# Sliding-window attention plus MLP on one core: attention in 64-key blocks on partition halves, 448 contracted as seven 64-row halves, a fixed queue order

## The chip, the cores and the metric

The kernel runs on one core of one Trainium2 chip. The metric is the device time of one execution in microseconds (us), lower is better. Each kernel was executed several times; "span" is the time from the first to the last instruction of the profiled execution, which lies 1.7 to 1.9 us under that execution's time where the record gives both. A run is called slow when it lies more than 1.5% above the fastest run of the same kernel; on one core nothing else tells such a run apart.

## The reference, cut to what matters

There are 2048 tokens of width 448 in bf16 and 16 heads of 28. Each query attends to eight keys: its own position and those 2, 4, ..., 14 behind it. So even and odd tokens never meet in attention. An MLP with token shifts of 1 and 2 follows, then a second MLP of width 1792.

```python
def _A_ref(x, wqkv, wo):                 # called with layernorm(x); H = 16, Dh = 28
    W, dil = 8, 2
    q, k, v = ...                        # x @ wqkv, split by heads
    idx = pos[:, None] - off[None, :]    # off = 0, 2, ..., 14
    logits = einsum("bhsd,bhswd->bhsw", q, kg) * Dh ** -0.5     # kg, vg gathered by idx
    attn = softmax(where(mask, logits, -1e9))
    return einsum("bhsw,bhswd->bhsd", attn, vg) @ wo

def _B_ref(x, w1, w2, w3, w4):           # called with layernorm(h)
    h = gelu(layernorm(x) @ w1)
    hs = concat(shift(h, quarters, by +1, -1, +2, -2)) @ w2
    x1 = x + hs
    return x1 + gelu(layernorm(x1) @ w3) @ w4      # w3: 448 x 1792, w4: 1792 x 448

h = x + _A_ref(layernorm(x), wqkv, wo)
out = h + _B_ref(layernorm(h), w1, w2, w3, w4)
```

## The kernel before

Tokens are cut into four tiles of 512 tokens of one parity. The contraction of 448 is four chunks of 112 rows, so each 512-column product is four matmuls that use 112 of the 128 rows. Attention works in blocks of 110 keys and 103 queries: five blocks per tile and head. The program first makes a graph of operations; a greedy list scheduler then decides, when the program is built, which operation each engine queue takes next.

```python
    def phase_QK(t):                     # phase_V is alike, 110 tokens a block
        for c in range(4):
            T = tile(2)
            for which in range(2):
                for kc in range(4):      # 4 x 112 rows
                    j0 = 16 * which + 4 * c
                    mm(T(...), wqk_p[:, kc, j0:j0 + 4, :]..., hT[0:KC, par, kc, :], kc == 0, kc == 3, 512)
            copy(qk[:, par, c, :, 8:520], T(...), 1024)

    def phase_att(t):
        for c in range(4):
            for jp in range(2):
                T = tile(2)
                for q0, nq, k0 in BLK:                        # five blocks of 103 queries, 110 keys
                    for j in (2 * jp, 2 * jp + 1):
                        mm(T(...), qk[32 * j:32 * j + 28, par, c, 1, k0:k0 + KB],
                           qk[32 * j:32 * j + 28, par, c, 0, 8 + q0:8 + q0 + nq], True, True, nq, "rows")
                pj = pt[0:KB, sl, 2 * jp:2 * jp + 2, :]
                act(pj, T(...), ACT.Exp, 1024, scale=SCALE)
                dve("tensor_tensor", 1024, 2.0, out=pj, in0=pj, in1=m_, op=ALU.mult)     # mask
            ...                                                # attention times V, 20 matmuls; evacuation
        # softmax denominators: gathered, inverted, stored, broadcast by DMA
        dma("zg%d" % par, zp[:, par, :], zrows, 32768)
        dve("reciprocal", 400, out=rzp[:, par, :], in_=zp[:, par, :])
        ...
        dma("zs%d" % par, zd..., rzp[:, par, :], 32768)
        for j in range(4):
            dma("zb%d" % j, rzb[32 * j:32 * j + 32, :, :]..., bass.AP(rz_d, ...), 32 * 8192)
        for c in range(4):
            dve("tensor_tensor", 512, out=oT[:, par, c, :], in0=osb[:, par, c, :], in1=rzb[:, c, :], op=ALU.mult)

    def schedule(self, dma_bw=180.0, slack=100.0):
        ...
        while done < n:                  # of all ready operations take the one that can start first
            for e in engs:
                for op in ready[e]:
                    st = max(avail(op, e), fr)
                    ...
                    if cand is None or st < cand[0] - slack or (st < cand[0] + slack and op.prio < cand[1].prio):
                        cand = (st, op)
```

## Time and profile before

| | before |
|---|---|
| median of 3 runs (lowest, highest) | 247.87 us (245.72, 248.72) |
| span of the profiled execution | 245.1 us |
| TensorE, VectorE, ScalarE busy | 205.1, 119.4, 122.3 us |
| matmuls | 1505 |
| bytes moved by DMA | 19.82 MB |

The page's first lines give busy time per engine. The rows of tenths cut the span into 40 slices of 6.1 us: 9 is 90% busy or more. PEclk is the clock granted to TensorE, in tenths. The trace's first clock record lies at 19.3 us here, and the page counts the time before it as full clock; the 9s at the head of this row are therefore no measurement. The q8 line is a queue whose packets the page calls instruction, 14 of them here.

```profile
PE 205.1 (84%) x1505; PEld 104.5 (43%) x1505; DVE 119.4 (49%) x237; ACT 122.3 (50%) x138; POOL 61.7 (25%) x123
PE   0389787899799759659782999999999999999990
PEclk9999979999999967959997699999999999999999
DMA  6910598950700774447044400046000401001110
...
q8 instruction: 14, 0.23, 0.4%
```

The groups of instructions, by form. After the count stand the total busy time in us, the mean of one in ns, then the engine's idle time just ahead and what ended it.

```profile
L1181 PE MATMUL ps<-hT,arena 112*128 112x512 bf16 x128 | 30.5, 395 | 1.0 <-ACT pt L1181 0.9
L1181 ACT ACTIVATE pt<-ps 110x1024 bf16<-110x1024 f32 x32 | 30.3, 1037 | 0.3 <-PE ps L1181 0.3
L1181 DVE TENSOR_TENSOR pt<-pt,msk 110x1024 bf16<-110x1024 bf16 x32 | 21.8, 697 | 12.0 <-ACT pt L1181 11.8
L1181 PE MATMUL ps<-qk 28*110 28x103 bf16 (+1 forms) x320 | 11.5, 227 | 6.4 <-ACT pt L1181 2.5
```

Matmuls overlap: one of the first line takes 395 ns on average, yet 25 of them from 48.91 us on start 216 ns apart and take 5.57 us in all. So a matmul's mean is not its pace: pace is the distance between starts. What TensorE waited for, by who released it, in us in total, times, longest:

```profile
PE ps L1181 <- ACT lntm L1181: 8.7, 3, 6.8
PE ps L1181 <- DVE oT L1181: 6.0, 5, 3.9
PE ps L1181 <- ACT pt L1181: 5.6, 10, 1.4
PE ps L1181 <- DMA actT<-lntm: 2.9, 2, 2.5
```

The timeline of TensorE at the two ends of what matters here (start in us, length in us, what, count, idle before it):

```profile
13.76 5.96 PE L1181 MATMUL ps<-arena,hT 112*110 112x448 bf16 x16 [1.11 <-ACT hT L1181]
...
135.27 17.44 PE L1181 MATMUL ps<-actT,w_s 112*128 112x512 bf16 x72 [2.52 <-DMA actT<-lntm]
```

"issue" is the page's word for a wait that nothing in the profile explains. TensorE's first large product (V of the first tile) starts at 13.76 us and runs at 5.96/16 = 372 ns a matmul, where the same form later takes 202 ns (3.23 us for 16 at 41.97 us). And between there and 135 us TensorE stands idle again and again for other engines, while from 135.27 us on it is nearly gapless.

### The profile page before, as it was taken

The numbers are of one execution on the slowest core, as the hardware profiler recorded it, in microseconds if no ns is written. First come the engines' busy times: TensorE is split into PE (matmuls) and PEld (weight loads), VectorE is DVE, ScalarE is ACT, GpSimd is POOL, SyncE is SP. The second block draws the span as 40 slices with busy tenths as digits, with TensorE's granted clock in tenths as the row PEclk, the third lists the DMA queues.
The fourth block names the chain that finished last, engine by engine and source line by source line (L and its number), as shares of the span: only waits on it lengthen the run. The fifth ranks groups of instructions, "written<-read, shape, count | busy, mean of one in ns | idle before, by whom it ended". The sixth has DMA issues, their size and how long they took to land.

```text
span 245.1 us, 3658 instructions
## 1 busy us (share of the span) xinstructions
PE 205.1 (84%) x1505; PEld 104.5 (43%) x1505; DVE 119.4 (49%) x237; ACT 122.3 (50%) x138; POOL 61.7 (25%) x123
## 2 busy tenths in 40 slices
PE   0389787899799759659782999999999999999990
PEld 0245333545445544415341354544454454445550
DVE  6456872165677797778799100773036122002221
ACT  2635865677955795861836565154615600650000
POOL 8830835010000500320539100286003600000000
PEclk9999979999999967959997699999999999999999
DMA  6910598950700774447044400046000401001110
GB/s 165 282 49 19 111 221 249 299 86 8 175 5 11 174 84 88 100 91 177 17 73 86 86 0 0 3 92 136 0 19 3 86 19 56 3 1 39 37 61 26
DMA packets 31671, 19.82 MB, mean 81 GB/s; under 512 B 24800, under 2 KB 30256, under 8 KB 31136
## 3 DMA queue, kind: packets, MB, share of 16 engines
q1 hardware_dynamic: 30608, 15.10, 29.0%
q0 software_dynamic: 1040, 4.42, 6.6%
q8 instruction: 14, 0.23, 0.4%
q14 instruction: 9, 0.07, 0.1%
HBM read 11.65 MB, written 1.97 MB: 56 GB/s over the span
## 4 chain that ended last, share of the span: by engine, by line
PE 61%; ACT 12%; DVE 10%; POOL 6%; DMA 6%; issue 2%; DVEq 0%
PE ps L1181 61%; ACT pt L1181 5%; DMA actT<-lntm 3%; DVE st L1181 3%; POOL rstd L1181 3%; DMA hT<-lntm 3%; ACT lntm L1181 3%; DVE oT L1181 2%; ACT arena L1181 2%; DVE xb L1181 2%; POOL nmr L1181 1%; ACT qk L1181 1%; ACT vt L1181 1%; DVE mv L1181 1%; DVE pt L1181 1%
## 5 line engine op out<-in xcount | busy, mean ns | idle before, releaser
L1181 PE MATMUL ps<-actT,w_s 112*128 112x512 bf16 (+1 forms) x288 | 65.5, 387 | 2.9 <-DMA actT<-lntm 2.9
L1181 ACT ACTIVATE arena<-ps 128x1024 bf16<-128x1024 f32 (+1 forms) x35 | 35.9, 1025 | 42.7 <-PE ps L1181 42.6
L1181 DVE TENSOR_TENSOR xb<-ps,xb 128x448 bf16<-128x448 f32 (+1 forms) x24 | 18.5, 771 | 75.0 <-PE ps L1181 75.0
L1181 PEld LDWEIGHTS ps<-actT,w_s 112*128 112x128 bf16 (+1 forms) x288 | 30.3, 107 | 35.8 <-DMA actT<-lntm 3.4
L1181 PE MATMUL ps<-w_s,arena 128*128 128x448 bf16 x224 | 43.0, 352 | 0.0
L1181 PE MATMUL ps<-hT,arena 112*128 112x512 bf16 x128 | 30.5, 395 | 1.0 <-ACT pt L1181 0.9
L1181 PEld LDWEIGHTS ps<-w_s,arena 128*128 128x128 bf16 x224 | 21.9, 98 | 20.6
L1181 ACT ACTIVATE pt<-ps 110x1024 bf16<-110x1024 f32 x32 | 30.3, 1037 | 0.3 <-PE ps L1181 0.3
L1181 POOL TENSOR_SCALAR vtmp<-mv 128x4 f32<-128x4 f32 (+1 forms) x19 | 3.8, 198 | 94.9 <-DVE mv L1181 93.9
L1181 DVE TENSOR_TENSOR pt<-pt,msk 110x1024 bf16<-110x1024 bf16 x32 | 21.8, 697 | 12.0 <-ACT pt L1181 11.8
L1181 PE MATMUL ps<-wo_s,oT 128*128 128x448 bf16 x64 | 17.2, 415 | 6.5 <-DVE oT L1181 6.0
L1181 PEld LDWEIGHTS ps<-hT,arena 112*128 112x128 bf16 x128 | 12.6, 101 | 16.5 <-issue 2.0
L1181 DVE BATCH_NORM_STATS2 st<-xin 128x6 f32<-128x448 bf16 x32 | 19.2, 599 | 0.5 <-issue 0.5
L1181 POOL TENSOR_TENSOR rstd<-vtmp,mhalf 128x4 f32<-128x4 f32 (+1 forms) x19 | 18.3, 962 | 1.6
L1181 PE MATMUL ps<-arena,hT 112*110 112x448 bf16 x64 | 15.6, 407 | 2.5 <-ACT qk L1181 1.4
L1181 PE MATMUL ps<-qk 28*110 28x103 bf16 (+1 forms) x320 | 11.5, 227 | 6.4 <-ACT pt L1181 2.5
L1181 POOL TENSOR_TENSOR xb<-xb,xin 128x448 bf16<-128x448 bf16 x16 | 16.2, 1040 | 2.3 <-ACT lntm L1181 1.7
L1181 ACT ACTIVATE lntm<-xin,nmr,rstd 128x448 bf16<-128x448 bf16 x16 | 11.3, 752 | 10.5 <-POOL nmr L1181 10.5
L1181 ACT ACTIVATE qk<-ps 128x1024 bf16<-128x1024 f32 x10 | 10.1, 1021 | 10.7 <-PE ps L1181 10.7
L1181 PEld LDWEIGHTS ps<-wo_s,oT 128*128 128x128 bf16 x64 | 6.7, 110 | 16.4 <-DVE oT L1181 8.8
L1181 ACT ACTIVATE lntm<-xb,nmr,rstd 128x448 bf16<-128x448 bf16 x11 | 7.7, 751 | 12.0 <-POOL nmr L1181 12.0
L1181 PEld LDWEIGHTS ps<-qk 28*110 28x110 bf16 x320 | 8.9, 134 | 10.7 <-ACT pt L1181 3.8
(58 smaller groups left out, 172.2 us busy)
## 6 DMA issues: line engine op xcount, KB each, us to landing
rzb<-rz_scratch SPq DMA_DIRECT2D x16, 256.0 KB, 4.6
w_s<-in_B_w_dram POOLq DMA_DIRECT2D x2, 1568.0 KB, 11.2
out_dram<-xb SPq DMA_DIRECT2D x16, 112.0 KB, 1.7
xin<-in_A_x_dram SPq DMA_DIRECT2D x3, 448.0 KB, 8.0
arena<-in_A_wqkv_dram SPq DMA_DIRECT2D x3, 392.0 KB, 5.5
w_s<-in_B_w_dram POOLq DMA_DIRECT2D x2, 392.0 KB, 7.5
xin<-in_A_x_dram SPq DMA_DIRECT2D x4, 112.0 KB, 2.2
wo_s<-in_A_wo_dram POOLq DMA_DIRECT2D x4, 98.0 KB, 3.2
```

Of the source, the lines that this page charges most:

```text
L1181: inst = getattr(eng, op.meth)(**op.kw)
```

## The change

The intent is to cut TensorE's work, to halve the number of exponentials and masks, and to fill the attention stage's gaps with MLP work.

- Chunks hold 512 consecutive tokens of both parities. Keys of one parity sit on partitions 0 to 63 and of the other on 64 to 127, so one exp and one mask serve both. Blocks have 64 keys and 51 queries.
- 448 rows are seven halves of 64. Four loads of 128 rows at offsets 0, 128, 192 and 320 put every half on the upper or lower partitions as needed, and 28 half matmuls on two tiles make four outputs.
- V goes through DRAM to reach the partitions of its blocks.
- The softmax of the first chunk is normalised on VectorE with 32x32 transposes instead of a DMA round trip.
- 14 dummy matmuls run during the first loads, and the loads come from two queues.
- The greedy scheduler is replaced by a table of 771 entries that a search outside the kernel found.

```diff
-    NST, NTL, KC, NF = 4, 16, 112, 14
-    BLK = [(103 * b, 103, 103 * b + 1) for b in range(4)] + [(412, 100, 410)]
-    KB = 110
+    NCH, NTL, G, NF = 4, 16, 112, 14
+    NB, QS, KS = 5, 51, 50
+    QB = [(0, QS + 1)] + [(QS * b + 1, QS) for b in range(1, NB)]
+    WIN = (0, 128, 192, 320)
+    TPE, FAST = (0, 1), (0,)
...
+    def quad(outs, lhsTs, rhss, n, T1, T2):
+        lo, hi = slice(0, 64), slice(64, 128)
+        def phase(a, b, ba, bb, first, T):
+            for x, y in zip(ba, bb):
+                mms.append((outs[a], lhsTs[a](lo, x), rhss[a](lo, x), ...))
+                mms.append((outs[b], lhsTs[b](hi, y), rhss[b](hi, y), ...))
+            ...
+        p1 = phase(0, 1, (0, 1, 2, 3), (0, 1, 2, 3), True, (g1, g2))
+        p2 = phase(2, 3, (0, 1, 2, 3), (0, 1, 2, 3), True, ())
+        p3 = phase(1, 0, (0, 1, 3), (0, 2, 3), False, ())
+        p4 = phase(3, 2, (0, 1, 3), (0, 2, 3), False, ())
...
+    tag("warm")
+    pe([(T(lambda p: p[:, 0, :]), zz[:, 0:128], zz[:], True, True)] * WARM, WARM * 330.0, "full")
...
+        for p in range(2):               # V to DRAM and back
+            dma("vw%d" % p, bass.AP(v_d, ...), vraw[:, 2 * p:2 * p + 2, :, :]..., 128 * 2 * 1024)
+            dma("vr%d%d" % (s, p), vt[64 * p:64 * p + 64, s, :, :, :]..., bass.AP(v_d, ...), 64 * NB * 1024)
...
+                for b, (q0, n) in enumerate(QB):
+                    for p in range(2):
+                        for j in range(4):
+                            mms.append((Ts[j // 2](...), qk[32 * j:32 * j + 28, s, 2 * g + u, 1, p, KS * b:KS * b + 64],
+                                        qk[32 * j:32 * j + 28, s, 2 * g + u, 0, p, 8 + q0:8 + q0 + n], True, True))
...
+    def norm_blocks(c, g, p, O):
+        dve("transpose", ..., out=t1, in_=O(lambda x: x[:, 0, :]))
+        dve("reciprocal", 255, out=rz, in_=v(t1)[:, :, 28])
+        dve("scalar_tensor_tensor", 690, out=v(tb), in0=v(t1), scalar=UP, in1=rz..., op0=ALU.mult, op1=ALU.mult)
+        dve("transpose", 690, out=heads(g)[:, p, :, :], in_=tb...)
...
-    def schedule(self, dma_bw=180.0, slack=100.0):
-        ... (greedy list scheduler)
+    def schedule(self, table):
+        for entry in table:              # name, engine a or v, PSUM banks
+            ...
+_ORDER = """ 4 0 18 3 14 17 19 2 1 15 61 20:7 60 76 68 8 12 62 16 69 ... """.split()
```

## The prediction

> What bounds the kernel now. The page gives TensorE 84% busy, VectorE 49%, ScalarE 50%; the chain that ended last is 61% TensorE. By the timeline, until 13.8 us TensorE runs only 28 transposes while the first layer norm is made; V(0) then runs at 372 ns a matmul against 202 ns for the same form later. From 135.3 to 239.5 us TensorE is gapless, 216 ns per 512-column and 189 ns per 448-column matmul. Tail 5.6 us. At these settled rates all its matmuls come to about 184 us: wide ones 171.5 (V 15.1, QK 27.6, WO 12.1, W1 13.8, W2 12.1, W3 48.4, W4 42.4), scores 6 (about 19 ns each in bursts of 20 and 30), attention-times-V 4.5 (14 ns), transposes 2. So some 61 of 245.1 us are head, tail, slow clock and gaps, about 40 of them between 20 and 135 us, where the chain alternates between exps (32 of 1.04 us), evacuations, layer-norm statistics and 4.3-4.6 us transposing DMAs.
>
> What the change does.
> 1. The 448-deep contractions use 64-row halves: 28 half passes make four outputs, 14 full passes where 16 were. [...]no run here has 64-row tiles yet. If halves overlap fully: QK -3.4, W1 -1.7, W3 -5.7, and V (20 passes to 14 per chunk) -4.5 us. Wide work falls from 171.5 to about 156 us.
> 2. Scores and AV go from 320+320 matmuls of 103 columns to 640+640 of 51 on eight tiles. From the old 14-19 ns I estimate 11-13 each: 15 us, +4.5. Exp halves (16 instead of 32 of 1.04 us, -16.6 us ScalarE), masks halve (-11 us VectorE).
> 3. Chunks hold 512 consecutive tokens of both parities: early MLP work fills attention's gaps. The first softmax is normalised by four VectorE chains (about 2.3 us each) instead of a DMA round trip; V pays a DRAM round trip, hidden behind QK.
> 4. Fourteen dummy matmuls during the initial loads, loads from two queues: V(0) should start near 9 us at full clock instead of 13.8 at half ([...]372 against 202 ns agrees). Worth 7 us.
> 5. A searched queue order replaces the greedy one.
>
> Useful TensorE work then is about 173 us (156 + 15 + 2). Head 9, tail 5.5, gaps, [...]slow clock 12 instead of 40: span 199.5 us; timed runs lie some 2.5 us above the profiled span: 202 us. Of 46 us saved, 11 are TensorE work, 7 head, 28 middle gaps. ScalarE and VectorE, under 120 us each, don't bound the whole.
>
> To see in the profile: V(0) before 10 us, clock 0.95 or better; half-pass matmuls about 108 ns apart for 512 columns; S and AV bursts of 80 in about 1 us; 16 exps of 1.04 us; W3 work before 75 us (before: 135 us); TensorE busy about 90% with few waits over 1 us between 20 and 190 us; last stretch gapless.
>
> What would make it wrong: halves that don't overlap (+16 us and more), small matmuls issue-bound at 18-20 ns (+8 to 10 us), [...]a fixed order that stalls when a DMA lands late (V round trip, broadcasts, weights), the last chunk's serial chain of two layer norms not covered by earlier groups' W4.

Head 9, TensorE work 173, tail 5.5 and 12 for gaps and slow clock make a span of 199.5 us, and with 2.5 us between span and timed runs 202 us. That dummy matmuls would bring the first product to full clock was the author's estimate, and so was that halves overlap; before's trace, with 372 and 202 ns, shows two paces and not what sets them. The other estimates come from before's trace: 108 ns is half of 216; the 18 to 20 ns among the risks is the pace of its scores (the bursts of 20 at 46.21 and 64.61 us start 18 and 20 ns apart); the 16 us matches the fall from 171.5 to 156. The 2.3 us of a VectorE chain agree with the trace after: 0.69, 0.22, 0.67 and 0.69 us for its four instructions.

## The result, and the profile after

| | before | after |
|---|---|---|
| median (lowest, highest) | 246.80 us (244.79, 248.72), 4 runs | 216.49 us (216.01, 217.86), 4 runs |
| ratio of fast runs | | 0.881, 95% interval 0.875 to 0.887 |
| span, granted clock | 245.1 us, 0.950 | 214.2 us, 0.973 |
| TensorE, VectorE, ScalarE busy | 205.1, 119.4, 122.3 us | 183.7, 120.5, 92.1 us |
| matmuls | 1505 | 2687 |
| bytes moved by DMA | 19.82 MB | 23.53 MB |

A ratio is the mean time of one kernel's fast runs over that of the other's in the same rounds, so it is not quite the ratio of the medians. Before has one more run here than in the section above.

The kernel is 12% faster, so the direction was right. But 216.49 us lies 14.5 us above the predicted 202, so the prediction was wrong in size. The granted clocks count the time before the first clock record as full, so both are somewhat too high, before's the more. The page after:

```profile
PE 183.7 (86%) x2687; PEld 99.9 (47%) x2687; DVE 120.5 (56%) x250; ACT 92.1 (43%) x111; POOL 52.5 (24%) x108
PE   7189998756994799779979897999999999999980
PEclk9759999999799999999999999999999999999998
DMA  5995949799199924940051870035400091000111
...
q8 instruction: 23, 0.38, 0.8%
```

The DMA row shows a 9 in nine of the first 14 slices (75 us; a slice is 5.4 us), where before had three in the first 12 (73 us). The groups:

```profile
L1236 PE MATMUL ps<-hT,arena 64*128 64x512 bf16 x224 | 28.0, 403 | 1.1 <-DVE hT L1236 0.5
L1236 ACT ACTIVATE pt<-ps 128x1024 bf16<-128x1024 f32 x16 | 15.5, 1023 | 6.5 <-PE ps L1236 6.5
L1236 DVE TENSOR_TENSOR pt<-pt,msk 128x1024 bf16<-128x1024 bf16 x16 | 11.7, 738 | 3.1 <-ACT pt L1236 3.1
...
L1236 PE MATMUL ps<-pt,vt 64*32 64x51 bf16 (+1 forms) x640 | 6.9, 190 | 5.5 <-issue 4.2
```

The exps and masks halved as planned: 16 of each, at 1.02 and 0.74 us (before 32 of each, at 1.04 and 0.70). But the last line has something new: 4.2 us of idle time before these small matmuls ended by "issue". The list of waits shows it as the largest item:

```profile
PE ps L1236 <- issue: 7.7, 6, 2.4
PE ps L1236 <- DVE lntm L1236: 4.6, 1, 4.6
PE ps L1236 <- DMA actT<-lntm: 3.6, 4, 1.6
PE ps L1236 <- ACT pt L1236: 2.8, 2, 2.4
```

One entry needs care. The 2.4 us put down to an exp (ACT pt) is the wait before matmul number 1142, counted from 0, the first of a group that reads the output of a transposing DMA. It ended at 67.83 us, 0.33 us after that exp and 0.20 us after that DMA had landed (67.63). In twelve further profiles, of the changed kernel and its variants, the same wait ends 0.20 us after this DMA landed, whether an exp ended 0.2 us before it or 2.4 (d0). So it is a wait for the DMA, which took 6.83 us here.

The timeline of TensorE in the head, then around 34 to 53 us:

```profile
1.25 4.92 PE L1236 MATMUL ps<-oT 128*128 128x512 bf16 x14 [1.25 <-DVE oT L1236]
10.73 2.10 PE L1236 MATMUL ps<-ident,lntm 128*128 128x128 bf16 x16 [4.56 <-DVE lntm L1236]
13.35 4.00 PE L1236 MATMUL ps<-hT,arena 64*128 64x512 bf16 x28 [0.52 <-DVE hT L1236]
17.19 2.81 PE L1236 MATMUL ps<-arena,hT 64*128 64x448 bf16 x28
19.93 0.83 PE L1236 MATMUL ps<-qk 28*64 28x52 bf16 x80
...
34.65 0.41 PE L1236 MATMUL ps<-qk 28*64 28x52 bf16 x33
35.86 0.55 PE L1236 MATMUL ps<-qk 28*64 28x51 bf16 x47 [0.80 <-issue]
36.34 1.47 PE L1236 MATMUL ps<-hT,arena 64*128 64x512 bf16 x12
37.74 0.71 PE L1236 MATMUL ps<-pt,vt 64*32 64x52 bf16 x69
39.59 0.23 PE L1236 MATMUL ps<-pt,vt 64*32 64x51 bf16 x11 [1.13 <-issue]
...
43.44 1.48 PE L1236 MATMUL ps<-wo_s,oT 128*128 128x448 bf16 x7
47.27 1.88 PE L1236 MATMUL ps<-wo_s,oT 128*128 128x448 bf16 x9 [2.35 <-issue]
```

Look at the counts. A burst of 80 score matmuls is cut into 33 and 47, a burst of 80 attention-times-V matmuls into 69 and 11, and a group of 16 output products into 7 and 9. The program waits for data once per operation, before its first matmul, and these stops fall inside an operation, so no data wait explains them. What happens at these points can be read from the individual DMA packets of the q8 queue, each of 16,384 bytes:

| instruction packet | TensorE stops before matmul number | its next start |
|---|---|---|
| 33.46 to 34.42 us | 475 | 35.86 us |
| 37.44 to 38.40 us | 603 | 39.59 us |
| 44.57 to 45.80 us | 729 | 47.27 us |
| 49.69 to 50.56 us | 856 | 52.02 us |
| 62.05 to 63.80 us | 1111 (0.3 us) | 65.07 us |
| 70.86 to 71.85 us | 1237 | 73.26 us |

The stops lie 126 to 128 matmuls apart, or twice that (856 to 1111). Each matmul has its weight load (the page counts 2687 of both), so 128 matmuls are 256 instructions of the queue: a block, in what follows. In each case TensorE resumes 1.2 to 1.5 us after a packet ended. The author's reading of this is that TensorE's instructions come in blocks of 256 with these packets, and that it stops where the next block comes late: a supply stop. The page doesn't say whose instructions a packet holds, so this is an inference. The number of packets agrees with it: TensorE's 2 x 2687 instructions are 21 times 256, and there are 23 packets; before had 2 x 1505, 11.8 times 256, and 14 packets; a1, with 432 matmuls fewer, has 19 packets and e2, with 336 more, 25. The six waits sum to 7.7 us.

The bookkeeping of the prediction against the measurement:

| term | predicted us | measured us | how |
|---|---|---|---|
| TensorE work at settled rates | 173 | 168.4 | wide 156 as predicted (half passes start 108 ns apart), bursts 10.4 instead of 15, transposes 2 |
| head | 9 | 13.4 | first large product starts at 13.35 |
| tail | 5.5 | 6.0 | TensorE ends at 208.2 |
| gaps, slow clock | 12 | 26.4 | what is left of 214.2 |
| span | 199.5 | 214.2 | |

The 10.4 us of bursts are 640 score matmuls at 8.3 ns and 640 attention-times-V matmuls at 7.9 ns, from bursts of 80 in 0.80 to 0.83 us of which about 0.17 us is the last one's own end. Of the 26.4 us, 18.1 are idle time between 13.35 and 208.2 us (that stretch less TensorE's busy time in it); the other 8.3 are busy time above the settled rates, that of slow clock among it. The trace's clock records show half clock from 8.20 to 15.02 us and from 52.57 to 55.98 us (in the clock row the 7 and 5 at the head, and the single 7 later). Of this 1.7 and 3.4 us lie in the busy stretch, so about 2.5 us of the 8.3 are slow clock, an estimate from half the time at half clock. The second fall follows the stops of 34 to 52 us and is absent in a3, which has fewer of them. The other 5.8 us no run here splits.

### The profile page after: what moved, and what is told of

Same layout as the page of the kernel before. It is cut to its first block, busy times and chain, and to the rows that moved or that the text cites. A ratio compares the mean times of both kernels' runs of the same rounds, so it can differ in the third digit from the quotient of the medians.

```text
span 214.2 us, 6051 instructions
## 1 busy us (share of the span) xinstructions
PE 183.7 (86%) x2687; PEld 99.9 (47%) x2687; DVE 120.5 (56%) x250; ACT 92.1 (43%) x111; POOL 52.5 (24%) x108
## 2 busy tenths in 40 slices
DMA packets 37568, 23.53 MB, mean 110 GB/s; under 512 B 22800, under 2 KB 36768, under 8 KB 37536
## 4 chain that ended last, share of the span: by engine, by line
PE 48%; DVE 18%; DMA 16%; issue 6%; ACT 4%; POOL 4%; SPq 2%; ACTq 0%
PE ps L1236 48%; DMA actT<-lntm 7%; DVE st L1236 5%; DVE xb L1236 5%; DMA rzb<-rz_scratch 4%; DMA arena<-in_A_wqkv_dram 3%; DVE lntm L1236 2%; DVE xin L1236 2%; ACT qk L1236 2%; SPq L1236 2%; DMA rz_scratch<-rzp 2%; POOL rstd L1236 1%; POOL xb L1236 1%; DVE oT L1236 1%; DVE mv L1236 1%
## 5 line engine op out<-in xcount | busy, mean ns | idle before, releaser
L1236 PE MATMUL ps<-actT,w_s 64*128 64x512 bf16 (+3 forms) x672 | 56.1, 323 | 6.7 <-DMA actT<-lntm 3.6
L1236 PEld LDWEIGHTS ps<-actT,w_s 64*128 64x128 bf16 (+1 forms) x672 | 34.5, 99 | 27.8 <-ACT arena L1236 3.3
L1236 ACT ACTIVATE arena<-ps 128x512 bf16<-128x512 f32 (+2 forms) x40 | 28.4, 766 | 17.3 <-PE ps L1236 17.3
L1236 PE MATMUL ps<-hT,arena 64*128 64x512 bf16 x224 | 28.0, 403 | 1.1 <-DVE hT L1236 0.5
L1236 PEld LDWEIGHTS ps<-hT,arena 64*128 64x128 bf16 x224 | 10.9, 100 | 16.0 <-issue 3.4
L1236 ACT ACTIVATE pt<-ps 128x1024 bf16<-128x1024 f32 x16 | 15.5, 1023 | 6.5 <-PE ps L1236 6.5
L1236 ACT ACTIVATE qk<-ps 128x1024 bf16<-128x1024 f32 x10 | 10.1, 1024 | 17.7 <-PE ps L1236 17.7
L1236 DVE SCALAR_TENSOR_TENSOR oT<-osb,rzb 128x512 bf16<-128x512 f32 x12 | 7.5, 686 | 14.8 <-DMA rzb<-rz_scratch 14.8
L1236 DVE TENSOR_TENSOR pt<-pt,msk 128x1024 bf16<-128x1024 bf16 x16 | 11.7, 738 | 3.1 <-ACT pt L1236 3.1
L1236 DVE SCALAR_TENSOR_TENSOR xin<-ps,xin 128x896 bf16<-128x896 f32 x8 | 8.6, 1073 | 8.2 <-PE ps L1236 8.2
L1236 PE MATMUL ps<-w_s,gT 112*128 112x448 bf16 x64 | 13.1, 353 | 0.0
L1236 PE MATMUL ps<-arena,hT 64*128 64x448 bf16 x112 | 11.4, 350 | 0.4 <-ACT qk L1236 0.4
```

The lines of the kernel that those rows point to most:

```text
L1236: inst = getattr(eng, meth)(**kw)
```

## The experiments

The edits are to the changed kernel unless said otherwise. Four groups ran, each on one chip: names with a, b, d and e. The groups a, d and e have a run of the changed kernel as control; b has none. The fast runs of the three controls average 216.9, 214.4 and 213.3 us, so between groups a few us mean nothing.

The theory after the result: DMA traffic is so dense up to 75 us that what TensorE waits for, its own instructions among it, lands late. Rivals: the gaps belong to the content (a slot or bank), the half passes lose more than they save, the head is the cause, or the order is.

### a0_change_again: the control

No edit.

> Control: the changed kernel once more, to be compared with its variants on the same chip. Expected 216 to 218 us, and again gaps of TensorE at every second or third boundary of 128 matmuls (256 queue instructions): before matmul 475, 603, 729, 856, 1237.

Measured: runs of 215.56 to 218.79 us, ratio 0.883; issue waits 8.1 us, before the same matmul numbers 475, 603, 729, 856 and 1237. These numbers repeat to the instruction, and the sixth stop, 0.2 us, comes before 1111 again, so they are no chance event.

### a1_full_passes: four full passes instead of seven halves

Wrong result: windows overlap, so rows are counted twice. A phase is now four matmuls of 128 rows for one output.

```diff
-        p1 = phase(0, 1, (0, 1, 2, 3), (0, 1, 2, 3), True, (g1, g2))
-        p2 = phase(2, 3, (0, 1, 2, 3), (0, 1, 2, 3), True, ())
-        p3 = phase(1, 0, (0, 1, 3), (0, 2, 3), False, ())
-        p4 = phase(3, 2, (0, 1, 3), (0, 2, 3), False, ())
+        p1 = phase(0, (g1, g2))
+        p2 = phase(2, ())
+        p3 = phase(1, ())
+        p4 = phase(3, ())
```

> Undoes the 64-row halves alone: four full 128-row passes per output over the same overlapping windows (rows 192 to 255 are counted twice, so the result is wrong on purpose), 16 passes in place of 14, everything else and the order kept. TensorE work rises by 12.5 us (QK 3.4, W1 1.7, V 1.5, W3 5.9). If TensorE bounds most of the span, the time rises by 9 to 13 us. Rival: if chains of latency bound the middle, only the last third (W3 of the last groups) pays, +4 to +6 us. The 432 fewer matmuls move the 128-matmul boundaries to other places: if the gaps come from instruction fetch they move with them.

Measured: two fast runs of 217.12 and 220.09 us, mean 218.6, against 216.9 for the control's fast runs; ratio 0.888 against 0.883. Two more runs, among them the profiled one, were slow. In that slow profile TensorE is busy 197.9 us, its issue waits are 2.2 us and there are 19 instruction packets instead of 23. So the half passes do save TensorE work, but only about 2 us of it reach the time, which is inside the noise (the intervals overlap) and far from the 9 to 13 us expected. The fewer instructions came with fewer issue waits, two instead of six; that this is what gives the saving back fits, but a slow profile alone can't prove it.

### a2_no_warmup: one dummy matmul of one column instead of 14 of 512

```diff
-    pe([(T(lambda p: p[:, 0, :]), zz[:, 0:128], zz[:], True, True)] * WARM, WARM * 330.0, "full")
+    pe([(T(lambda p: p[:, 0, 0:1]), zz[:, 0:128], zz[:, 0:1], True, True)], 64.0, "full")
```

> The fourteen dummy matmuls become one of one column. Theory: they are of no use, since 4.6 us of idle follow them and the clock is low again when the first projection runs: 0 +- 0.7 us. Rival (the prediction's): they save the cold start, so without them +3 to +6 us. Instruction-fetch theory: every gap stays at the same count of matmuls, so the first one moves from after 33 of 80 score matmuls to after 46 of 80 of the same burst.

Measured: fast runs 213.74 and 212.88 us (control 216.9); two more of 217.25 and 216.46 are slow. The warm-up gains nothing, and may cost a little. In this profile QK of the first chunk takes 5.20 us instead of 4.00, so the dummies do shorten that one product by 1.2 us, but the time isn't shorter for it. More telling: with 13 matmuls fewer ahead, stops remain before matmul numbers 475, 603 and 856 (0.8, 0.8 and 3.0 us), which are now other matmuls. They follow the count, not the content.

### a3_light_dma: the same instructions, fewer bytes

Wrong result: weights w3 and w4, the reciprocals' broadcast and V's read are cut to a part, 15.96 MB instead of 23.53. Instruction counts stay at 6051.

```diff
-            win_load("w3%d" % h, w3_s[:, :, h * H:(h + 1) * H], B_w3[:, h * H:(h + 1) * H], 512 * F, ("sp", "sp"))
+            win_load("w3%d" % h, w3_s[:, :, h * H:h * H + 128], B_w3[:, h * H:h * H + 128], 512 * F, ("sp", "sp"))
...
-            dma("w4%d" % k, w4_s[:, f0:f1, :], w4v[:, f0:f1, :], (f1 - f0) * 128 * D * 2)
+            dma("w4%d" % k, w4_s[:, f0:f0 + 1, :], w4v[:, f0:f0 + 1, :], (f1 - f0) * 128 * D * 2)
...
-                bass.AP(rz_d, 8192 * c + 1024 * j, [[0, 32], [4096, 2], [1, 1024]]), 32 * 8192, bw=220.0)
+                bass.AP(rz_d, 8192 * c + 1024 * j, [[0, 32], [512, 4], [1, 64]]), 32 * 8192, bw=220.0)
...
-                bass.AP(v_d, (p * VROW + 256 * c) * 512, [[512, 64], [KS * 512, NB], [1, 512]]), 64 * NB * 1024)
+                bass.AP(v_d, (p * VROW + 256 * c) * 512, [[512, 64], [KS * 512, 1], [1, 512]]), 64 * NB * 1024)
```

> Same instructions on every engine, fewer bytes: w3, w4, the broadcasts of the reciprocals and the reads of V back from DRAM carry 64 to 128 columns or one block in place of all (wrong on purpose), about 7.5 of 23.5 MB less. Theory (instruction fetch and transposing DMAs are delayed by a full DMA): TensorE's gaps without a wait fall from 7.7 us to under 3 us, transposing DMAs land in 4.5 in place of 6.8 us, and the span falls by 8 to 13 us. Rival (gaps come from mode changes, semaphores or small matmuls themselves): the gaps stay, span -0 to -4 us.

Measured: 204.49 to 205.26 us, all four runs fast, ratio 0.832 (interval 0.828 to 0.836): 12.1 us under the control. TensorE is as busy as before (182.7 us). The waits of this kernel:

```profile
PE ps L1236 <- DVE lntm L1236: 4.2, 1, 4.2
PE ps L1236 <- issue: 2.4, 2, 1.5
PE ps L1236 <- DVE pt L1236: 1.8, 2, 0.9
PE ps L1236 <- DMA actT<-lntm: 1.7, 4, 1.0
```

And the stretch from 34 to 74 us, first of the changed kernel, then of this one. After the window and its length stand the busy times of PE, PEld, DVE, ACT and POOL with counts, then the granted clock, the DMA engines' busy share and GB/s.

```profile
34.00:74.00 40.00, 29.45 (x895) 16.39 (x891) 25.51 (x46) 20.83 (x23) 3.66 (x10) 0.96 0.87 190
```

```profile
34.00:74.00 40.00, 36.20 (x954) 19.96 (x949) 32.98 (x58) 22.56 (x25) 4.81 (x13) 1.00 0.49 99
```

With the DMA engines 49% busy instead of 87%, TensorE works 6.75 us more in the same 40 us. Issue waits fall by 5.3 us. Waits for transposing DMAs, with the one before matmul 1142 counted among them, fall by 3.4 us (6.0 to 2.6); that DMA now lands in 4.99 us instead of 6.83. The stop before matmul 603 remains (1.53 us), in a place where 128 matmuls, most of them small, last only 2.4 us (from 475 at 35.86 us to 602 at 38.26 us in the changed kernel). So traffic is shown to cost about 12 us. By the lists of waits, instruction supply is the largest single way in which it does between these two profiles (5.3 of the 11.3 us by which the spans differ), and late transposing DMAs the second; a smaller part of the stops needs no heavy traffic. The instruction packets take 0.9 to 1.8 us each in both kernels, so what differs is when they start. Why they start late beside dense data no run here shows.

### b1_greedy_order: the change's operations in a greedy order

The table was made with the algorithm and constants of before's scheduler, the priority being the order in which the program lists its operations.

```diff
-_ORDER = """ 4 0 18 3 14 17 19 2 1 15 61 20:7 60 76 68 8 12 62 16 69 ...
+_ORDER = """ 2 0 18 1 14 16 17 19 4 3 60 15 20:7 61 59 6 5 63 62 64 ...
```

> The same operations and buffers as the changed kernel, but queue order and banks from a greedy list scheduler like that of the kernel before (with the change's own durations) in place of the searched table. If the searched order carries much of the gain (the prediction gave 28 us of 46 to closed gaps): 228 to 245 us. If order matters little: 216 to 224 us.

Measured: 267.93 to 269.99 us, ratio 1.092: slower than before, and above the expected 228 to 245. The page's clock is 0.879, and the waits are

```profile
PE ps L1237 <- DMA actT<-lntm: 21.5, 3, 10.1
PE ps L1237 <- DVE fbit L1237: 7.5, 1, 7.5
PE ps L1237 <- issue: 6.3, 4, 2.4
```

The searched order is worth about 52 us against this order. One caution: in the changed kernel up to 80 matmuls are placed as one operation, whereas before's scheduler moved single matmuls, and a greedy order with tuned priorities could do better. The run shows that the work saved by the new blocking does not by itself make the kernel faster.

### b2_greedy_dma_softmax: as b1, and the first softmax by DMA too

```diff
-    TPE, FAST = (0, 1), (0,)
+    TPE, FAST = (0, 1), ()
```

> As b1, and the first chunk's softmax is normalised by the DMA round trip like the other three chunks. To be compared with b1 only. Theory: the four VectorE chains (9.3 us of VectorE) spare a round trip of some 12 us in a full DMA at the point where nothing else is ready: b2 slower than b1 by 4 to 10 us. Rival: TensorE has other work there, 0 +- 2 us.

Measured: 281.73 to 285.42 us, ratio 1.148; the fast runs' mean is 14.1 us above b1's, more than the expected 4 to 10. The waits for transposing DMAs rise to 36.7 us. The round trip of the expectation took 12.3 us at its shortest in before's trace (from 57.04 us, the issue of its first DMA, to 69.34 us), and the four chains are busy for 9.1 us in the changed kernel's. In the greedy order the 32x32 transposes are worth that much, as far as two greedy tables of different operations can be compared. What they are worth in the searched order stays open, since that table belongs to the other set of operations.

### b3_head_order: the first queue entries reordered

The first normalisations and transposes go ahead of the copies of the weights, which wait for a load until 8.26 us.

```diff
-... 9 70 5 64 11 71 29 93 65 27 13 66 23 28 75 30 67 21 59 31 32 24 73 22 48a 47v ...
+... 5 70 9 64 11 71 29 27 28 30 93 65 13 31 32 23 21 24 22 25 26 39 42 43:7 40:4 36 ...
```

> Only the order of the first layer norm's operations in the queues of VectorE, ScalarE, GpSimd and the DMA queue is changed: no weight copy stands before the four normalisations (it waits 1.7 us for a late load), the inverse deviations go before the mask setup, and the projection weights are issued before the second chunk of x. Theory: transposes start at about 7 in place of 10.7 us, QK(0) at 10 to 10.5 in place of 13.4 us and at full clock, the later stages are bound by TensorE and the queue order, so 2 to 4 us less in all. Rival: the middle absorbs it, 0 to -1 us.

Measured: 215.27 to 216.40 us, all fast, ratio 0.875. The head of its timeline:

```profile
7.04 0.62 PE L1237 MATMUL ps<-ident,lntm 128*128 128x128 bf16 x8 [1.07 <-DVE lntm L1237]
...
12.46 5.92 PE L1237 MATMUL ps<-hT,arena 64*128 64x512 bf16 x28 [1.83 <-DVE hT L1237]
18.23 2.81 PE L1237 MATMUL ps<-arena,hT 64*128 64x448 bf16 x28
```

The transposes start 3.7 us sooner, at 7.04 instead of 10.73 us. Yet QK starts only 0.9 us sooner and takes 5.92 us instead of 4.00, so V starts a microsecond later than in the changed kernel. The clock was low again (half from 11.19 to 18.02 us by the clock records), although the transposes ran in between. Whether they have any part in it this trace can't show: they are busy for only 1.4 of the 6.5 us between the dummies and QK. The expected gain of 2 to 4 us is not there, so far as a group without a control can tell: this order of the head's queues doesn't mend the prediction's miss.

### b4_light_v: only V's read cut

Wrong result. One of five blocks is read; 21.43 MB in all.

```diff
-                bass.AP(v_d, ..., [[512, 64], [KS * 512, NB], [1, 512]]), 64 * NB * 1024)
+                bass.AP(v_d, ..., [[512, 64], [KS * 512, 1], [1, 512]]), 64 * NB * 1024)
```

> Only the read of V back from DRAM is cut to one of five blocks (wrong on purpose), 2.1 of the 7.5 MB that the light kernel saved. Theory: bytes of the DMA in the stretch 20 to 75 us matter whatever they belong to: 3 to 5 us of the 12 us, TensorE's gaps without a wait fall from 8 to about 5 us. Rival (prediction: the round trip is hidden behind QK): 0 to -1 us.

Measured: fast runs 213.09, 212.09 and 212.12 us, ratio 0.8625. Against b3 on the same chip, whose fast runs average 215.8 us, that is 3.4 us less. So the round trip of V is probably not wholly hidden. But the intervals of the two ratios overlap, b3 is itself an edited kernel, and b4 has two slow runs (216.97 and 216.74), so a cost of a few us is likely and not shown. The profiled run was slow and isn't used.

### d0_change_control, d1_light_weights, d2_late_weights

d0 has no edit. d1 cuts w3 and w4 as in a3. d2 keeps every byte and issues five of the w3 and w4 loads later in the queue, between the broadcasts that are needed sooner:

```diff
-... 177 103 152 153 ... 97 131 ... 135 299 96 204 ... 472 102 247 100 352 ...
+... 177 152 153 ... 131 ... 135 299 204 ... (96 97 after 311, 100 102 after 482, 103 after 101)
```

> Control on this chip: the changed kernel once more, unedited. Expected 215 to 218 us.

> Only the loads of w3 and w4 are cut (to the first 128 columns or one block of each part, wrong on purpose), about 2.6 of the 7.5 MB. All instructions stay. Theory (bytes count, whatever they belong to): 4 to 6 us of the 12 us of the light kernel, the gaps without a wait between 34 and 53 us shrink, those at 62 to 74 us stay. Rival (the reciprocals' broadcasts or the V reads alone matter): 0 to -1 us.

> Correct. Five weight loads (1.9 MB) move down the DMA queue out of the crowded stretch: two quarters of w3 from 33 and 38 us to about 54 us, three parts of w4 from 22 and 67 us to about 76 and 94 us. Theory: -1.5 to -4 us if they land in time, TensorE's gaps without a wait 8 to about 5 us. Rival: the stretch stays full because other transfers follow, 0 +- 1 us; if w3 comes late, a wait for it at 87 us.

Measured: d0 213.10 to 216.01 us in three fast runs (one slow), issue waits 8.7 us. d1 211.53 to 213.88, ratio 0.865 against 0.870 for d0: 1.5 us by the means of the fast runs, where 4 to 6 were expected. d2 213.14 to 215.30, ratio 0.868, issue waits 8.8: no gain, where 1.5 to 4 us were expected. So early weight loads are at most a small part of the loss, and moving these five does nothing.

The issue waits of d0 and d2 are not all supply. Of each, one wait (4.5 and 4.0 us) is the wait for the transposing DMA before matmul 1142, which the profile could not name here. The stops at block boundaries are 4.2 us in d0, 4.8 in d2 and 5.4 in d1: between profiles of the unedited kernel they differ by 4 us (8.1 in a0), and in this pair cutting the weights did not shorten them. d1 was passed as correct though most of its w3 and w4 is never loaded: the last MLP's share of the output is too small for the tolerance, so a pass says little about that branch.

### d4_late_bf16_nowarm: late loads, bf16 reciprocals, no warm-up

d2's order, a2's missing warm-up, and the reciprocals stored and broadcast in bf16, so half the bytes. The result is correct.

```diff
-    rzb = sb("rzb", [128, 4, 512], F32)
-    rzp = sb("rzp", [128, 2, 64], F32)
-    rz_d = nc.dram_tensor("rz_scratch", (NCH * 8, 1024), F32, kind="Internal")
+    rzb = sb("rzb", [128, 4, 512], BF16)
+    rzp = sb("rzp", [128, 2, 64], BF16)
+    rz_d = nc.dram_tensor("rz_scratch", (NCH * 8, 1024), BF16, kind="Internal")
```

> Correct within the tolerance, I expect. As d2, and the reciprocals are stored and broadcast as bf16 (1.5 MB less), and the warm-up is one matmul of one column. Theory: 1 to 3 us less than d2; 210 to 214 us. Rival: no gain over d2.

Measured: fast runs 209.32, 211.60 and 209.34 us, one slow; ratio 0.853 against 0.870. The means of the fast runs differ by 4.3 us.

### e0_change_control and e1_light_reciprocals

The last group ran to split the cost of traffic and to test the instruction supply directly. e0 has no edit; e1 cuts the broadcasts of the reciprocals alone, as in a3 (wrong result).

> Control on this chip for the three others: the changed kernel once more, unedited. Expected 213 to 218 us, 8 us of gaps without a wait.

> Only the broadcasts of the reciprocals are cut to 64 of 512 columns (wrong on purpose), about 2.7 of the 7.5 MB. If the parts of the light kernel add up (12 us in all, about 4 for the V reads and 2 for the weights), this one gives 4 to 6 us: the broadcasts stand in the chain before the second, third and fourth output projection and delay the transposing DMA at 61 us. Rival (the parts overlap): 1 to 3 us.

Measured: e0 has one run of 211.72 us and so four of its six runs (215.91 to 219.68) count as slow; the ratio given is 0.8755 (0.869 to 0.882), while its two fast runs average 213.3. e1: fast runs 207.78, 210.16 and 210.56 us, ratio 0.854 (0.847 to 0.862). So the broadcasts' bytes cost 3.8 us by the fast means and 5.3 by the ratios. Over the fast runs of before on this chip (mean 247.2) these two would give 0.863, so the given ratio doesn't rest on them alone. Issue waits are 7.9 us in e0 and 4.6 in e1, both profiled in fast runs, but 3.8 of e0's are the wait before matmul 1142 again. The stops at block boundaries are 4.1 and 4.6 us, so in this pair the cut did not shorten them; what came sooner is that transposing DMA, which landed after 4.66 instead of 6.36 us.

The parts then are V about 3.4, weights about 1.5, reciprocals 3.8 to 5.3: 9 to 10 us of a3's 12.1. Each alone is near the spread between groups. Only a3's whole is firmly shown.

### e2_more_instructions: the same bytes and work in 336 more matmuls

V and QK do each half pass as two matmuls of half the columns. The result is correct.

```diff
+                for h in range(2 if split else 1):      # left and right half of the columns
+                    ...
-             [lambda r, w: wv_s[r, w, :]] * 4, D, T1, T2)
+             [lambda r, w: wv_s[r, w, :]] * 4, D, T1, T2, split=True)
-                 [lambda r, w: hT[r, s, :, w, :]] * 4, 512, T1, T2)
+                 [lambda r, w: hT[r, s, :, w, :]] * 4, 512, T1, T2, split=True)
```

> Same DMA bytes, same arithmetic: every half-pass matmul of the projections (V, QK) is split into two of half the columns, 336 matmuls (672 queue instructions) more, all before 90 us; TensorE work +0.5 us. Instruction-fetch theory: a block of 256 instructions lasts less long while its successor comes through a full DMA, so the gaps without a wait grow from 8 to 11 to 16 us and the time by 3 to 8 us. Rival (the gaps are caused by late data, mode changes or the small matmuls): +0 to +1 us.

Measured: fast runs 218.65, 218.33 and 221.48 us, ratio 0.884 (0.876 to 0.891): 2.1 us above e0 by the ratios, whose intervals overlap, and 6.2 by the means of the fast runs; every fast run of e2 lies above both of e0's. The profiled run was a slow one (228.15 us), so its durations aren't compared; where it stopped can still be read:

```profile
PE ps L1242 <- issue: 15.3, 9, 3.2
```

Eight of these nine waits come before matmul numbers 603, 731, 858, 1112, 1367, 1493, 1620 and 2254, all in the middle of a group of equal matmuls: 126 to 128 apart or a multiple of that (2254 is five blocks after 1620), just as in the changed kernel, though the matmuls at these numbers are others. The one at 1620 falls inside the W2 products, where the changed kernel has none. And there are 25 instruction packets instead of 23. A rival that ties the stops to data or banks can't give this. The added matmuls' own cost is small where nothing stops them: 56 of 256 columns take 3.23 us here (at 28.73 us) and 28 of 512 columns 3.20 us in the changed kernel (at 26.31 us), which makes about 0.4 us for 336, an estimate. What share of the added 2 to 6 us is supply stays open.

### e3_best: d4 again, more rounds

The same kernel as d4.

> The version with late weights, bf16 reciprocals and no warm-up again (the same file as d4), in more rounds beside the control. Expected 209 to 212 us and 1.5 to 2.5 per cent below the control of the same chip; if d4's gain was chance, within 1 per cent of it.

Measured: five fast runs from 208.42 to 211.21 us (a sixth, 211.70, just counts as slow), ratio 0.851 (0.845 to 0.857), correct. Its interval doesn't meet e0's (0.869 to 0.882). By the ratios it is 2.8% under the change, by the means of the fast runs (209.8 against 213.3) 1.6%. Its waits, led by the idle head that no dummies fill:

```profile
PE ps L1237 <- DVE lntm L1237: 9.5, 1, 9.5
PE ps L1237 <- issue: 4.5, 3, 2.8
PE ps L1237 <- DMA actT<-lntm: 3.2, 3, 1.5
```

Simply moving 1.6 MB less and leaving out the warm-up beats both kernels: 15% under before. Since d2 alone gained nothing, the gain comes from the other two.

## Why the prediction was wrong in size, point by point

1. **The half passes: right in rate, less right in worth.** Starts are 108 ns apart for 512 columns, as predicted, and wide work is 156 us. But in a1 putting the full passes back costs only about 2 us, not clear of noise. By the prediction's own terms it should have cost 12.3 (QK 3.4, W1 1.7, W3 5.7, and 1.5 for V, as 16 passes against 14).
2. **Small matmuls: better than predicted.** 8.3 and 7.9 ns instead of 11 to 13: 10.4 us instead of 15.
3. **Exps and masks: right.** 16 of 1.02 us. They account for 14.8 of the 30.2 us by which ScalarE's busy time fell. The masks took 10.1 us off VectorE, whose whole did not fall all the same (119.4 to 120.5). As predicted, neither engine bounds the whole.
4. **"Head 9": wrong by 4.4 us.** The first large product starts at 13.35 us, not before 10 at full clock (it is QK; V follows at 17.19). The step that failed is "Fourteen dummy matmuls ... loads from two queues ... Worth 7 us". The chain in the head goes through a weight load that is issued at 1.71 us and lands at 8.26 (DMA engines are 83% busy up to 13.35 us). The dummies end at 6.17 us and the next work comes at 10.73, and in that pause the clock fell to half: by the clock records it is half from 8.20 to 15.02 us, and the third digit of the clock row is 5. The dummies' own starts are 427 ns apart until 4.64 us and 215 ns from 4.93 us, so their pace doubled while they ran, but QK at 13.35 us still began at half clock. (The fall came 2.0 us after the last dummy here and 5.4 us after it in a0; these runs show no fixed time for it.) In a2 and b3 neither leaving out the dummies nor another queue order of the head costs or saves what the prediction gave them.
5. **"V pays a DRAM round trip, hidden behind QK": probably wrong, by some 3 us** (b4; not clear of noise).
6. **"Gaps, ... slow clock 12 instead of 40": the step that failed most.** They measure 26.4, so 14.4 us were missed: as much as the whole miss of 14.5 us, since the head's +4.4 and the bursts' −4.6 cancel, by luck. The prediction took before's list of waits and asked which of them the new order would fill. Its list of risks names stalls when a DMA lands late, but its sum has no term for them, and instruction supply is not in it at all. There are two causes, and they act together. The change moves 23.53 MB instead of 19.82 and crowds it before 75 us; cutting bytes to 15.96 MB gives back 12 us (a3). As that is less than before moved, not all of the 12 is due to what the change added; how much is stays open. And it nearly doubles TensorE's instructions, in bursts where a block can last only 2.4 us (from matmul 475 to 602); issue waits, of which TensorE's list in before has none, come to 7.7 us; a3, at the same instruction count, has 2.4. In the three controls the boundary stops are 8.1, 4.2 and 4.1 us, so this part varies between profiles and a3's gain in it is 1.7 to 5.7 us. Late transposing DMAs are the second item, 3.4 us of a3's difference.
7. **W3 before 75 us: wrong, 87.0.** It follows from 4 to 6. The last stretch is gapless as predicted, from 146 us on TensorE is busy 61.4 of 61.9 us.
8. **The order.** It was the fifth point of the prediction and carried no number of its own. b1 shows that without it the rest of the change loses 9%.

What also stays open: what the 5.8 us of busy time beyond slow clock are, and why instruction packets start late.

## What to carry to other kernels

When a change turns few large matmuls into many small ones, count instructions as well as array time, and look where the small ones come in bursts while DMA is dense: here TensorE stopped six times between 34 and 74 us, with the DMA engines 87% busy, 126 to 128 matmuls or twice that apart and for 7.7 us in all. When a sum has the form "the gaps shrink from 40 to 12", list the new waits that the change makes (bytes added, and when; instruction packets; loads on the head's chain) with the same care as the old ones it fills. And test traffic by cutting bytes at the same instruction count before arguing about order: it is one edit, and here it moved the time by 12 us, where moving weight loads and reordering the head moved it by nothing that stands out. And when the profile says "issue", look whether a transfer landed just before the wait ended.
